# Transposes of x, dispatch and combine weights moved from TensorE to VectorE blocks and DMAs inside SBUF, in a kernel of attention and a soft mixture of experts

## The chip, the cores and the metric

The kernel runs on one core of one Trainium2 chip. The time is that of one execution on the device, in microseconds (us). All data are float32. A core has five engines that matter here: TensorE (PE, matrix products and transposes, results to PSUM), VectorE (DVE), ScalarE (ACT), GpSimd (POOL, hardly used) and SyncE (SP), whose queue starts all DMAs of this kernel.

## The reference

Attention without a softmax over 8 batches, and then a soft mixture of experts over all 19,968 tokens at once:

```python
scores = z @ z.transpose(0, 2, 1) / S              # B=8, S=2496, z has 64 columns
x = u * (np.maximum(scores, 0) ** 2 @ v)           # [8, 2496, 256] -> [19968, 256]
logits = x @ phi                                   # 32 slots: 8 experts of 4
d = softmax of logits over the tokens (axis 0)     # dispatch
slot_input = d.T @ x                               # [32, 256]
slot_out[e] = np.maximum(slot_input[e] @ w1[e], 0) @ w2[e]   # 256 -> 1024 -> 256
c = softmax of logits over the slots (axis 1)      # combine
out = c @ slot_out                                 # [19968, 256]
```

## The kernel before

**Attention loop.** The loop at L556 runs over 8 batches, 5 chunks of queries (four of 512 tokens and one of 448; the last batch starts with the 448 and ends with two of 256), and 5 steps of four key tiles (128 keys each). A step has two half-steps. `between(s)` (L560) opens a half-step: it takes one item from the list `work` (from the third half-step of a chunk on), then calls `pair` (L466), which issues the loads that are due and the scores of one pair of key tiles. `attend` (L215) follows with 24 matmuls into `acc` (22 and 20 in the last step, whose last key tile is half full).

**Scores and splits.** `scores` (L177) makes 6 matmuls into two PSUM tiles `sc` (a pool of two), since products of float32 are put together from high and low parts. ACT takes a relu of each into a tile `r` (a pool of four) and squares it there; DVE copies `r` rounded to `ph`, and subtracts: `pl` = `r` - `ph`. The tiles `ph` and `pl` (pools of ten) are what `acc` consumes. After the first 14, scores run three half-steps ahead of the `acc` matmuls that use them. The raw z and v of the next batch are loaded in the third to fifth chunk of a batch, and split into high and low parts by ACT and DVE a little later, in the lists `behind` (after the splits of a half-step) that `scores` runs.

**Groups.** When a chunk ends, `finish_chunk` (L263) multiplies `acc` by u into `xg` (x, features by tokens). At every 1024 tokens it adds a group, the generator `groups(q)` (L296), to `work`: 19 groups in the loop. A group makes the logits `lg` on PE, adds the slot sums of the group before (`late`), makes `L` (logits) and `E` (their exponentials, for dispatch) by DVE and ACT, turns x in 32 PE transposes of 64x64 (`turn_x`, L281, two items, copied to `xt` by ACT) and then L and E in 8 transposes (`le`). From `le` DVE and ACT make the combine weights `cw`; `slot_sums` (L381) multiplies the turned E by `xt`. Each group's slot sums are made with the logits of the next one; the last group of the loop (q = 18) makes its own.

**Order.** PE, ACT and DVE run in the order in which the program is written: their instructions go through `InOrder` (L42), so that each of them shows L50 as its line. SP's DMAs are called directly on `nc.sync`, and a scheduler places them.

**End.** In the last three half-steps `between_last` (L523) turns `cw` of 24 blocks (`cT`, L414 and L516) and the first part of the last 512 tokens' x. Behind the loop come the last 512 tokens, 15 transposes of the other `cw` blocks between them as fillers, the expert layers (`layer1`, `layer2`), and `tokens` (L818), which makes the output and sends it by DMA.

Of the kernel before, what the change touches and what calls it, by code (L numbers as in the profile page):

```python
# [53 lines left out]
def attn_soft_moe_kernel(ctx, tc, uT, v, zz, phi, ww, outT):  # L54
    nc = tc.nc

    pe, act, dve = (InOrder(tc, x) for x in (nc.tensor, nc.scalar, nc.vector))
# [17 lines left out]
    def load_z(b, j):  # L75
        if b == 0:
            raw = cw[:, 19 + 4 * j : 23 + 4 * j].rearrange("p g n -> p (g n)")
        else:
            raw = raws.tile([P, 512], F32, tag="raw", name=f"zr_{b}_{j}", bufs=NRAW)
        nc.sync.dma_start(raw, zz[b, :, j * 512 : (j + 1) * 512])  # L80
        zraw[b, j] = raw

        def split():
            t = zt[b, j] = blk.tile([P, 2, 512], F32R, tag="blk", name=f"z_{b}_{j}")
            for h in (1, 0):
                rows = HALF[h]
                act.copy(t[rows, h], raw[rows])
                dve.tensor_sub(t[rows, 1 - h], raw[rows], f32(t[rows, h]))

        return split  # L90

    def load_v(b, i):
        raw = raws.tile([P, 2, D], F32, tag="raw", name=f"vr_{b}_{i}", bufs=NRAW)
        nc.sync.dma_start(raw, v[b, :, 2 * i : 2 * i + 2, :])
# [27 lines left out]

    xt = xpool.tile([P, 2, 4, D], F32, name="xt")
# [3 lines left out]
    def constants():  # L127
# [13 lines left out]
        nc.sync.dma_start(phi_sb, phi.rearrange("(c p) s -> p c s", p=P))  # L141
# [35 lines left out]
    def scores(b, ch, p, w):  # L177
# [85 lines left out]
    def finish_chunk(b, ch, acc):  # L263
# [3 lines left out]
        while s < n:  # L267
# [13 lines left out]
    def turn_x(ps, x, j, ts):  # L281

        for t in ts:
            for c in range(2):
                for h, rows in enumerate(HALF):
                    pe.transpose(
                        ps[:, h, t * P + c * 64 : t * P + (c + 1) * 64],
                        x[rows, c, (4 * j + t) * P : (4 * j + t + 1) * P], ident[rows, rows],
                    )
        t = slice(ts[0], ts[-1] + 1)  # L290
        act.copy(
            xt[:, j, t].rearrange("p t (h k) -> p h t k", h=2),
            ps.rearrange("p h (t k) -> p h t k", k=P)[:, :, t],
        )

    def groups(q):  # L296
# [38 lines left out]
        yield  # L335
        if q == NQG - 2:

            yield

        for j in range(2):  # L340
            ps = ms_ps.tile([P, 2, 512], F32, tag="ms", name=f"tr_{q}_{j}")
            turn_x(ps, x, j, range(4))
            yield

        ps = ms_ps.tile([P, 2, 512], F32, tag="ms", name=f"le_{q}")
        for k, m_ in enumerate((L, E)):
            for j in range(2):
                for h, rows in enumerate(HALF):
                    o = (2 * k + j) * 64
                    pe.transpose(  # L350
                        ps[:, h, o : o + 64], m_[rows, j * P : (j + 1) * P], ident[rows, rows]
                    )
        le = wk.tile([P, 2, 2, P], F32, tag="le", name=f"le_{q}")
        lx, px = le.rearrange("p k j (h b) -> p h (k j) b", h=2), ps.rearrange("p h (k b) -> p h k b", b=64)
        act.copy(lx, px[:, :, 0:4])
        rm = wk.tile([P, 2, 8], F32, tag="rm", name=f"rm_{q}")
        lt = le[:, 0].rearrange("p j (t s) -> p (j t) s", s=NS)
        cg = cw[:, 2 * q : 2 * q + 2]
        cs = cg.rearrange("p j (t s) -> p (j t) s", s=NS)
# [4 lines left out]
        def combine():  # L364
            dve.tensor_reduce(rm[:, 0], lt, axis=AX.X, op=ALU.max)
            dve.tensor_sub(cs, lt, spread(0))
            middle.append(combine_exp)

        def combine_exp():
            act.activation(cg, cg, AF.Exp)  # L370
            begin.append(combine_sum)

        def combine_sum():
            dve.tensor_reduce(rm[:, 1], cs, axis=AX.X, op=ALU.add)
            dve.tensor_scalar_add(rm[:, 1], rm[:, 1], 1e-9)
            dve.reciprocal(rm[:, 1], rm[:, 1])
            dve.tensor_mul(cs, cs, spread(1))

        begin.append(combine)

        def slot_sums(ps):  # L381
            for j in range(2):
                for t in range(4):
                    e = le[:, 1, j, t * NS : (t + 1) * NS]
                    for h, rows in enumerate(HALF):
                        pe.matmul(
                            ps[t * NS : (t + 1) * NS, h, 0:D], e[rows], xt[rows, j, t],
# [18 lines left out]


        if q < NQG - 2:
            late.append(slot_sums)
            return  # L410
        yield
        slot_sums(ms_ps.tile([P, 2, 512], F32, tag="ms", name=f"sl_{q}"))

    def turn(k, ps):  # L414

        for i in range(min(8, NG - 8 * k)):
            for h, rows in enumerate(HALF):
                pe.transpose(ps[h][:, i * 64 : (i + 1) * 64], cw[rows, 8 * k + i], ident[rows, rows])
# [3 lines left out]
    def halves(t, g=8):  # L422
        return t[:, :g].rearrange("p g (h n) -> p h g n", h=2)

    def split_hi(k, px):
        n = min(8, NG - 8 * k)
        hi = blk.tile([P, 8, P], F32R, tag="blk", name=f"ch_{k}")
        act.copy(hi[:, :n], px[:, :n])
        parts[k] = hi, px

    def split_lo(k):
        n = min(8, NG - 8 * k)
        hi, px = parts[k]
        lo = blk.tile([P, 8, P], F32R, tag="blk", name=f"cl_{k}")
        dve.tensor_sub(lo[:, :n], px[:, :n], f32(hi[:, :n]))
        parts[k] = hi, lo


    def load_w(pool, tag):
        i = len(w_raw)  # L440
        if i < NW:
            t = pool.tile([P, 2, 512], F32, tag=tag, name=f"w_{i}")
            nc.sync.dma_start(t, ww[i].rearrange("p (k n) -> p k n", k=2))
# [5 lines left out]
    def load_u(b, ch):  # L449
# [3 lines left out]
        nc.sync.dma_start(  # L453
# [62 lines left out]
    def turn_out(k, ps):  # L516

        turn(k, ps)
        c8 = cw[:, 8 * k : 8 * k + 8]
        for h, copy in enumerate((act.copy, dve.tensor_copy)):  # L520
            copy(halves(c8)[:, h], ps[h].rearrange("p (g n) -> p g n", g=8))

    def between_last(k):  # L523
# [3 lines left out]
        if k:  # L527
            turn_x(xps[0], xg_[NQG - 1], 0, range(k - 1, k))
        if k == 1:
            ps = acc_ps.tile([P, 2, QC], F32, tag="acc", name="cT_1")  # L530
            turn_out(1, [ps[:, h] for h in range(2)])
        else:
            turn_out(k, [sc_ps.tile([P, QC], F32, tag="sc", name=f"cT_{k}_{h}") for h in range(2)])
# [65 lines left out]
    L = wk.tile([P, 2 * P], F32, tag="L", name="L_last", bufs=1)[:, 0:P]  # L599
    E = wk.tile([P, 2 * P], F32, tag="E", name="E_last", bufs=1)[:, 0:P]  # L600
    nc.gpsimd.memset(tiny[:, 0:512], 0.0)
# [7 lines left out]

    turned = [acc_ps.tile([P, 2, QC], F32, tag="acc", name="cT_3")]  # L610
    fills = iter(range(14))

    def turn_c8(i):
        pe.transpose(
            turned[i // 8][:, i // 4 % 2, i % 4 * P : (i % 4 + 1) * P], cw[:, 24 + i], ident
        )

    def fill(n):
        for i in [next(fills) for _ in range(n)]:
            turn_c8(i)  # L620
# [5 lines left out]
    def turn_c(c):  # L626

        for t in range(2):
            pe.transpose(xq[:, c, t * P : (t + 1) * P], x[:, c, (2 + t) * P : (3 + t) * P], ident)

    def copy_c(c):
        act.copy(
            xt[:, 0, 2:4].rearrange("p t (h c q) -> p t h c q", h=2, c=2)[:, :, :, c],
            xq[:, c, 0 : 2 * P].rearrange("p (t h q) -> p t h q", t=2, h=2),
        )
# [11 lines left out]
    turn_c(0)  # L647
    turn_c(1)
# [3 lines left out]
    act.activation(E, lg[:, 0:P], AF.Exp, bias=mneg[:, 0:1])  # L652
    copy_c(0)
    copy_c(1)
    dve.tensor_copy(L, lg[:, 0:P])
# [5 lines left out]
    fill(2)  # L661
    ps = acc_ps.tile([P, 2, QC], F32, tag="acc", name="et_last")
    turned.append(ms_ps.tile([P, 2, 512], F32, tag="ms", name="cT_4"))
    pe.transpose(ps[:, 0, 0:P], E, ident)
    act.copy(ET, ps[:, 0, 0:P])

    act.activation(fac, mneg, AF.Exp, scale=-1.0, bias=mtop)
    fill(3)
    lT = pm[:, P : 2 * P].rearrange("p (t s) -> p t s", s=NS)
    pe.transpose(pm[:, P : 2 * P], L, ident)  # L670
    fill(3)
    for t in range(4):
        pe.matmul(
            ps[t * NS : (t + 1) * NS, 1, 0:D], ET[:, t * NS : (t + 1) * NS], xt[:, 0, t],
            start=True, stop=True,
        )
    act.copy(snew[:, 0:D], ps[:, 1, 0:D])
    dve.tensor_reduce(snew[:, D : D + 1], E, axis=AX.X, op=ALU.add)
    dve.tensor_mul(
        fsel, ssel.unsqueeze(1).to_broadcast([P, 2, NS]), fac.unsqueeze(2).to_broadcast([P, 2, NS])  # L680
    )


    sums = [lg[:, 2 * P : 2 * P + NS], ps[:, 0, 2 * P : 2 * P + NS]]
# [8 lines left out]
    fill(2)  # L693

    cg = cw[:, NG - 1]
    cs = cg.rearrange("p (t s) -> p t s", s=NS)
# [4 lines left out]
    dve.tensor_reduce(rm[:, 0], lT, axis=AX.X, op=ALU.max)  # L701
    dve.tensor_sub(cs, lT, spread(0))
    slots(snew, 0)
    for c in range(2):
        dve.tensor_copy(
            sT[:, c, :, 0:SE], sums[c].rearrange("p (e s) -> p e s", s=SE)
        )
    act.activation(cg, cg, AF.Exp)


    tot = pm[:, 2 * P : 2 * P + NS]
# [6 lines left out]
    dve.tensor_reduce(rm[:, 1], cs, axis=AX.X, op=ALU.add)  # L718
    dve.tensor_scalar_add(rm[:, 1], rm[:, 1], 1e-9)
    dve.reciprocal(rm[:, 1], rm[:, 1])  # L720
    dve.tensor_mul(cs, cs, spread(1))
# [44 lines left out]
    whole = [cw[:, 8 * k : 8 * k + 8] for k in range(3)]  # L766
    whole += [t.rearrange("p h (g n) -> p (h g) n", n=P) for t in turned]
    hs = {}
    split_hi(3, whole[3])
    for i, k in enumerate((0, 1, 2, None)):  # L770
# [129 lines left out]
```

## Time and profile before

| | |
|---|---|
| median of 3 runs | 1495.19 us (1494.81 to 1495.38) |
| profiled execution | 1497.05 us |
| its span in the trace | 1495.1 us |
| end of the last `acc` matmul of the loop | 1418.6 us into the span |
| mean granted TensorE clock | 0.986 |

The page's slices show where the stages lie. Each digit is the busy share of one fortieth of the span (37.4 us) in tenths, and PEclk is the granted TensorE clock in tenths:

```profile
PE   9999999999999999999999999999999999999985
DVE  6878776887678777787778787687767787676754
ACT  7777766867567766777667766686767777665653
PEclk9999999999999999999999999999999999999995
DMA  4112201121001110121101120011101131000589
```

The loop fills 38 of the 40 slices. The last one and a half are the tail, in which the DMAs of the output are busiest. In the list of waits a row names who waits, for whom, the total in us, how often, and the longest; in a timeline a row has the start, the length, the engine, the line, the operation with output and inputs, and in brackets the idle time ahead of it with what ended it. A group's row has the total busy time and the mean in ns behind the first bar, and the idle time of the engine just ahead of it behind the second.

### The profile page before, as it was taken

To read this page: it belongs to the slowest core of one execution; us is meant where nothing else is said; L and a number is where in the kernel's file an instruction comes from. 1 tells how busy PE (TensorE), PEld (TensorE's weight loads), DVE (VectorE), ACT (ScalarE), POOL (GpSimd) and SP (SyncE) were. 2 spreads that over 40 slices of the span, in tenths; PEclk is the share of its full clock that TensorE was granted. 3 is DMA by queue.
4 is the path that set the end of the run, shared out by engine and by line. 5 is a ranking of instruction groups with operands and counts; after the bars stand their busy time and mean duration, and the time that the engine had idled before them with its cause. 6 is when DMAs were issued, how large, how long until landed. Compare 5 with 4: busy or idle time off the path is not lost.

```text
span 1495.1 us, 36884 instructions
## 1 busy us (share of the span) xinstructions
PE 1468.8 (98%) x14763; PEld 1247.3 (83%) x14763; DVE 1108.0 (74%) x2194; ACT 1025.1 (69%) x1982; POOL 3.7 (0%) x22
## 2 busy tenths in 40 slices
PE   9999999999999999999999999999999999999985
PEld 7888888889888888889988888888988889988952
DVE  6878776887678777787778787687767787676754
ACT  7777766867567766777667766686767777665653
POOL 0000000000000000000000000000000000000000
PEclk9999999999999999999999999999999999999995
DMA  4112201121001110121101120011101131000589
GB/s 133 31 30 58 55 24 29 30 64 57 16 23 51 50 42 15 30 55 51 30 16 43 52 70 16 15 51 49 51 16 30 51 112 56 16 16 23 191 317 388
DMA packets 36651, 91.53 MB, mean 61 GB/s; under 512 B 3712, under 2 KB 6272, under 8 KB 34432
## 3 DMA queue, kind: packets, MB, share of 16 engines
q1 hardware_dynamic: 36480, 89.18, 18.9%
q8 instruction: 116, 1.90, 0.6%
q14 instruction: 55, 0.45, 0.1%
HBM read 68.71 MB, written 20.45 MB: 60 GB/s over the span
## 4 chain that ended last, share of the span: by engine, by line
PE 97%; DMA 1%; ACT 1%; DVE 0%; issue 0%; SPq 0%; ACTq 0%; DVEq 0%
PE acc L50 71%; PE sc L50 19%; PE lg L50 2%; PE tr L50 1%; PE pf L50 1%; DMA outT<-ot 1%; PE po L50 1%; ACT ot L50 1%; PE h L50 0%; DMA vr<-in_v 0%; PE le L50 0%; PE cT L50 0%; DVE ot L50 0%; PE idle L50 0%; PE hT L50 0%
## 5 line engine op out<-in xcount | busy, mean ns | idle before, releaser
L50 PE MATMUL acc<-ph,v 64*128 64x512 f32 (+2 forms) x6396 | 1012.9, 381 | 0.4 <-issue 0.4
L50 PEld LDWEIGHTS acc<-ph,v 64*128 64x128 f32 x6396 | 653.2, 184 | 91.3 <-issue 0.8
L50 ACT ACTIVATE r<-sc 128x512 f32<-128x512 f32 (+2 forms) x820 | 429.1, 575 | 357.7 <-PE sc L50 351.7
L50 PE MATMUL acc<-pl,v 64*128 64x512 f32 (+2 forms) x3198 | 669.2, 380 | 0.0
L50 DVE TENSOR_TENSOR pl<-r,ph 128x512 fp32r<-128x512 f32 (+5 forms) x820 | 546.4, 666 | 68.3 <-PE acc L50 0.9
L50 DVE CAST ph<-r 128x512 fp32r<-128x512 f32 (+2 forms) x820 | 335.6, 409 | 249.5 <-ACT r L50 247.6
L50 ACT ACTIVATE r<-r 128x512 f32<-128x512 f32 (+2 forms) x820 | 454.9, 610 | 0.0
L50 PEld LDWEIGHTS acc<-pl,v 64*128 64x128 f32 x3198 | 347.2, 184 | 46.1
L50 PE MATMUL sc<-z,z 64*128 64x512 f32 (+2 forms) x1920 | 277.0, 384 | 0.2 <-ACT r L50 0.2
L50 PEld LDWEIGHTS sc<-z,z 64*128 64x128 f32 x1920 | 186.9, 185 | 32.5 <-issue 6.6
L50 PE MATMUL sc<-z 64*128 64x512 f32 (+2 forms) x480 | 69.9, 386 | 0.0
L50 DVE TENSOR_TENSOR v<-vr,v 128x512 fp32r<-128x512 f32 x80 | 54.9, 686 | 5.6 <-ACT v L50 5.2
L50 ACT COPY xt<-tr 128x1024 f32<-128x1024 f32 x38 | 38.6, 1016 | 27.2 <-PE tr L50 27.1
L50 PEld LDWEIGHTS sc<-z 64*128 64x128 f32 x480 | 47.0, 185 | 7.0 <-issue 1.6
L50 ACT CAST v<-vr 128x512 fp32r<-128x512 f32 x80 | 49.4, 617 | 3.7 <-DMA vr<-in_v 3.7
L50 DVE TENSOR_TENSOR xg<-acc,ut 128x1024 f32<-128x1024 f32 (+7 forms) x57 | 48.8, 880 | 1.2 <-PE acc L50 1.2
L50 DVE TENSOR_TENSOR z<-zr,z 64x512 fp32r<-64x512 f32 x70 | 48.0, 686 | 2.0
L50 ACT CAST z<-zr 64x512 fp32r<-64x512 f32 x70 | 43.4, 620 | 1.7
L50 DVE COPY ot<-pf 128x1024 f32<-128x1024 f32 (+2 forms) x22 | 24.3, 1104 | 23.1 <-PE pf L50 21.4
L50 ACT COPY ot<-pf 128x1024 f32<-128x1024 f32 (+2 forms) x22 | 20.1, 915 | 27.3 <-PE pf L50 22.4
L50 PE MATMUL pf<-ch,soh 32*128 32x512 f32 (+2 forms) x88 | 23.1, 570 | 12.4 <-ACT ot L50 12.4
L50 PEld LDWEIGHTS pf<-ch,soh 32*128 32x128 f32 x88 | 10.2, 244 | 23.1 <-ACT ot L50 22.1
(129 smaller groups left out, 449.1 us busy)
## 6 DMA issues: line engine op xcount, KB each, us to landing
vr<-in_v SPq DMA_DIRECT2D x80, 256.0 KB, 2.7
w<-in_w SPq DMA_DIRECT2D x32, 512.0 KB, 6.4
outT<-ot SPq DMA_DIRECT2D x16, 1024.0 KB, 7.0
ut<-in_uT SPq DMA_DIRECT2D x31, 512.0 KB, 3.7
zr<-in_zz SPq DMA_DIRECT2D x35, 256.0 KB, 2.7
ut<-in_uT SPq DMA_DIRECT2D x8, 448.0 KB, 3.5
outT<-ot SPq DMA_DIRECT2D x4, 512.0 KB, 4.5
outT<-ot SPq DMA_DIRECT2D x2, 768.0 KB, 7.2
```

Source lines behind the costliest of these rows:

```text
L50: return lambda *a, **k: self.tc.keep_in_program_order(f(*a, **k))
```

## The change

PE makes none of the loop's transposes any more, nor those of `cw`. DVE's transpose turns each 32x32 block of a tile in its place within a row of blocks, and 16 small DMAs (`shift`) then carry the blocks from one quarter of the partitions to another. This is done to E (tile `e1`, shifted to `es`) and to each half of x (tile `y`, a single buffer that both halves use in turn, shifted to `xt`). The logits are turned by DVE alone into `lt`; the combine softmax is made there in another order of tokens, and a second DVE transpose puts the result back into `cw`, in the layout that the end needs, so `turn`, `turn_out` and `turn_c8` go. A group now takes 8 items of `work` in place of 7 (14 for q = 18). The tiles `e1`, `es`, `lt` and `y` are new, and the pool of `r` has three buffers in place of four. SP's DMAs go through `InOrder` too, so they are issued in program order. Rows of w1 are permuted on the host to fit the new order of features.

```diff
-    pe, act, dve = (InOrder(tc, x) for x in (nc.tensor, nc.scalar, nc.vector))
+    pe, act, dve, sp = (InOrder(tc, x) for x in (nc.tensor, nc.scalar, nc.vector, nc.sync))
...
-            r = wa.tile([P, QC], F32, tag="r", name=f"r_{t0}_{k0 + h}", bufs=4)
+            r = wa.tile([P, QC], F32, tag="r", name=f"r_{t0}_{k0 + h}", bufs=3)
...
-                work.extend([lambda it=it: next(it, None)] * 7)
+                work.extend([lambda it=it: next(it, None)] * (14 if q == NQG - 2 else 8))
...
+    def shift(dst, src, n):
+        for a in range(4):
+            for b in range(4):
+                sp.dma_start(
+                    dst[32 * b : 32 * b + 32, a * n : (a + 1) * n],
+                    src[32 * a : 32 * a + 32, b * n : (b + 1) * n],
+                )
...
-        for j in range(2):
-            ps = ms_ps.tile([P, 2, 512], F32, tag="ms", name=f"tr_{q}_{j}")
-            turn_x(ps, x, j, range(4))
-            yield
-        ps = ms_ps.tile([P, 2, 512], F32, tag="ms", name=f"le_{q}")
...
-                    pe.transpose(
-                        ps[:, h, o : o + 64], m_[rows, j * P : (j + 1) * P], ident[rows, rows]
-                    )
...
+        e1 = wk.tile([P, 2 * P], F32, tag="e1", name=f"e1_{q}", bufs=1)
+        es = wk.tile([P, 2 * P], F32, tag="es", name=f"es_{q}", bufs=1)
+        def turn_e():
+            dve.transpose(
+                e1.rearrange("p (b j s) -> p j b s", b=4, j=2), E.rearrange("p (j b k) -> p j b k", j=2, b=4)
+            )
+            shift(es, e1, 64)
+        behind.append(turn_e)
         yield
...
+        def turn_block(y, j, c):
+            dve.transpose(
+                y.rearrange("p (b t c f) -> p c t b f", b=4, t=4, c=2)[:, c],
+                x[:, c, 512 * j : 512 * (j + 1)].rearrange("p (t b k) -> p t b k", t=4, b=4),
+            )
+            if c:
+                shift(xt[:, j].rearrange("p t d -> p (t d)"), y, D)
...
         def combine():
-            dve.tensor_reduce(rm[:, 0], lt, axis=AX.X, op=ALU.max)
-            dve.tensor_sub(cs, lt, spread(0))
-            middle.append(combine_exp)
+            dve.transpose(lt, L)
+            dve.tensor_reduce(rm[:, 0], l8, axis=AX.X, op=ALU.max)
+            dve.tensor_sub(l8, l8, spread(0))
...
+        def combine_turn():
+            dve.transpose(cw[:, 2 * q : 2 * q + 2].rearrange("p j n -> p (j n)"), lt)
...
+                            es[rows, o : o + NS],
+                            xt[rows, j].rearrange("p g (t n) -> p t g n", t=4)[:, t],
...
+        for j in range(2):
+            y = wk.tile([P, 2 * QC], F32, tag="y", name=f"y_{q}_{j}", bufs=1)
+            for c in range(2):
+                behind.append(lambda: turn_block(y, j, c))
+                if j:
+                    middle.append(combine_exp) if c == 0 and not short else None
+                yield
+            if j == 0:
+                if not short:
+                    behind.append(combine)
+                yield
+        if not short:
+            behind.append(combine_sum)
+            behind.append(combine_turn)
             late.append(slot_sums)
             return
...
-            turn_out(k, [sc_ps.tile([P, QC], F32, tag="sc", name=f"cT_{k}_{h}") for h in range(2)])
+            turn_x(xps[0], xg_[NQG - 1], k - 1)
+            copy_x(act.copy, xps[0], k - 1)
...
+    def fill(n, ps=ep_):
+        for _ in range(n):
+            pe.transpose(ps[:, 1, 0:P], ident, ident)
...
+    dve.transpose(cw[:, NG - 1], lt)
...
-    w1 = inputs["moe_w1"].reshape(2, 4, 2, 2, 64, 2, 512).transpose(0, 5, 3, 1, 2, 4, 6)
+    w1 = inputs["moe_w1"].reshape(2, 4, 2, 2, 2, 32, 2, 512).transpose(0, 6, 3, 1, 4, 2, 5, 7)
```

Three places of the order, all in the chunk that works off the first group. On PE before, the transposes of x stand between two half-steps (`acc` matmuls of key tile 7, then `tr`, then the scores of tiles 14 and 15):

```order
L50 MATMUL acc_1190<-pl_7_1213,v_3_272 128x512 x2
L50 MATMUL tr_0_1415<-ident,xg_691 128x64 x16
L50 MATMUL sc_14_1433<-z_2_568,z_3_665 128x512
L50 MATMUL sc_15_1434<-z_2_568,z_3_665 128x512
...
L50 MATMUL acc_1190<-ph_8_1255,v_4_321 128x512 x4
```

On PE now the same place has nothing between them:

```order
L50 MATMUL acc_1190<-pl_7_1213,v_3_272 128x512 x2
L50 MATMUL sc_14_1437<-z_2_568,z_3_665 128x512
L50 MATMUL sc_15_1438<-z_2_568,z_3_665 128x512
...
L50 MATMUL acc_1190<-ph_8_1255,v_4_321 128x512 x4
```

The row of 16 transposes is gone. On DVE now, from half-step 5 (key tiles 16 and 17) to half-step 7 (key tiles 0 and 1 of the next chunk), `y_0` and `y_1` being the two halves of the group's x in the same buffer:

```order
L50 STREAM_TRANSPOSE y_0_1436<-xg_691 128x4x4x32
L50 TENSOR_TENSOR z_1_1460<-zr_1_1240,z_1_1460 64x512 x2
L50 CAST ph_16_1505<-r_16_1500 128x512
...
L50 STREAM_TRANSPOSE y_0_1436<-xg_691 128x4x4x32
L50 CAST ph_18_1569<-r_18_1564 128x512
...
L50 STREAM_TRANSPOSE lt_1434<-L_1306 128x256
...
L50 TENSOR_TENSOR pl_1_1635<-r_1_1624,ph_1_1633 128x512
L50 STREAM_TRANSPOSE y_1_1611<-xg_691 128x4x4x32
L50 CAST ph_2_1676<-r_2_1671 128x512
```

The transposes stand behind the splits of one half-step and ahead of the first cast of the next, where before there were only splits, sums and subtractions; the first `y_1` row writes the buffer that the DMAs of `y_0` read. On SP now, from the last load ahead of the group to the first load behind it (`zr` and `vr` are z and v of the next batch, `ut` is u):

```order
L50 DMA zr_2_1368<-in_zz 128x512
L50 DMA es_1367<-e_0_1366 32x64 x16
L50 DMA zr_3_1490<-in_zz 128x512
L50 DMA xt<-y_0_1436 32x256 x16
L50 DMA zr_4_1612<-in_zz 128x512
L50 DMA xt<-y_1_1611 32x256 x16
L50 DMA vr_0_1730<-in_v 128x512
L50 DMA ut_1783<-in_uT 128x2x512
```

Three shifts of 16 DMAs have come between the loads, which stood directly behind each other there before; loads behind a shift in this queue are issued after it.

More of the change, by code (lines that the diff above doesn't have):

```diff
@@ L140, in constants @@
                 )
-        nc.sync.dma_start(phi_sb, phi.rearrange("(c p) s -> p c s", p=P))
+        sp.dma_start(phi_sb, phi.rearrange("(c p) s -> p c s", p=P))
         nc.gpsimd.memset(one, 1.0)
@@ L514, in attn_soft_moe_kernel @@
     xps = []
[L516 to L521, printed above, removed]
     def between_last(k):
@@ L607, in attn_soft_moe_kernel @@
     dve.tensor_scalar_mul(mneg[:, 1:2], mold, -1.0)
[L610 to L620, printed above, removed]
     lg = sc_ps.tile([P, QC], F32, tag="sc", name="lg_last")
@@ L624, in attn_soft_moe_kernel @@
     xq = ms_ps.tile([P, 2, 512], F32, tag="ms", name="tr_last_1")
[L626 to L635, printed above, removed]
+    ep_, tp = (acc_ps.tile([P, 2, QC], F32, tag="acc", name=n) for n in ("et_sums", "et_last"))
+    def fill(n, ps=ep_):
+        for _ in range(n):
+            pe.transpose(ps[:, 1, 0:P], ident, ident)
     def logits(c):
@@ L660, in attn_soft_moe_kernel @@
     )
[L661 to L665, printed above, removed]
+    pe.transpose(tp[:, 0, 0:P], E, ident)
+    act.copy(ET, tp[:, 0, 0:P])
     act.activation(fac, mneg, AF.Exp, scale=-1.0, bias=mtop)
-    fill(3)
-    lT = pm[:, P : 2 * P].rearrange("p (t s) -> p t s", s=NS)
-    pe.transpose(pm[:, P : 2 * P], L, ident)
+    dve.transpose(lt, lg[:, 0:P])
+    dve.tensor_mul(
+        fsel, ssel.unsqueeze(1).to_broadcast([P, 2, NS]), fac.unsqueeze(2).to_broadcast([P, 2, NS])
+    )
     fill(3)
@@ L692, in attn_soft_moe_kernel @@
     slots(sold, 1)
[L693 to L696 removed]
+    fill(2, tp)
+    l4 = lt.rearrange("p (b s) -> p b s", s=NS)
     def spread(i):
         return rm[:, i].unsqueeze(2).to_broadcast([P, 4, NS])
[L701 to L702 removed]
+    dve.tensor_reduce(rm[:, 0], l4, axis=AX.X, op=ALU.max)
+    dve.tensor_sub(l4, l4, spread(0))
     slots(snew, 0)
[L704 to L711, printed above, removed]
+    for c, copy in enumerate((dve.tensor_copy, act.copy)):
+        copy(sT[:, c, :, 0:SE], sums[c].rearrange("p (e s) -> p e s", s=SE))
+    act.activation(lt, lt, AF.Exp)
+    tot = tp[:, 0, 2 * P : 2 * P + NS]
     for z, k in (sold, 1), (snew, 0):
@@ L763, in layer2 @@
                 )
-    whole = [cw[:, 8 * k : 8 * k + 8] for k in range(3)]
-    whole += [t.rearrange("p h (g n) -> p (h g) n", n=P) for t in turned]
     hs = {}
-    split_hi(3, whole[3])
-    for i, k in enumerate((0, 1, 2, None)):
-        if k is not None:
-            split_hi(k, whole[k])
-        split_lo((3, 0, 1, 2)[i])
+    split_hi(0)
+    for i in range(4):
+        if i < 3:
+            split_hi(i + 1)
+        split_lo(i)
         hs[divmod(i, 2)] = layer1(*divmod(i, 2))
```

118 lines of the change are left out of this document (46 added, 72 removed).

## The prediction

> **What bounds the kernel now.** I read the page's engine line first, then the busy time by stage, then the chain that ended last.
>
> ```profile
> PE 1468.8 (98%) x14763; PEld 1247.3 (83%) x14763; DVE 1108.0 (74%) x2194; ACT 1025.1 (69%) x1982; POOL 3.7 (0%) x22
> 200.00:600.00 400.00, 400.00 (x3882) 339.10 (x3880) 298.69 (x589) 277.46 (x532) 0.00 (x0) 1.00 0.13 35
> PE 97%; DMA 1%; ACT 1%; DVE 0%; issue 0%; SPq 0%; ACTq 0%; DVEq 0%
> ```
>
> TensorE (PE) is busy 400.00 of 400.00 us at a granted clock of 1.00, and holds 97% of the chain. A TensorE instruction that goes is a saving, as long as the engines that feed it stay ahead. How far ahead they are decides this case, so the next rows are one beat of the loop: PE from the chain, then ScalarE (ACT), then VectorE (DVE).
>
> ```profile
> 382.06 0.69 PE sc L50 x6
> 382.76 2.79 PE acc L50 x24
> 385.55 0.69 PE sc L50 x6
> 382.57 1.09 ACT L50 ACTIVATE r<-sc 128x512 f32<-128x512 f32 x2 [1.35 <-PE sc L50]
> 383.54 1.15 ACT L50 ACTIVATE r<-r 128x512 f32<-128x512 f32 x2
> 384.21 0.43 DVE L50 CAST ph<-r 128x512 fp32r<-128x512 f32 x1 [1.12 <-ACT r L50]
> 384.74 0.69 DVE L50 TENSOR_TENSOR pl<-r,ph 128x512 fp32r<-128x512 f32 x1
> 385.35 0.42 DVE L50 CAST ph<-r 128x512 fp32r<-128x512 f32 x1
> 385.87 0.69 DVE L50 TENSOR_TENSOR pl<-r,ph 64x512 fp32r<-64x512 f32 x1
> ```
>
> A half-step (hs) is 3.49 us (382.06 to 385.55). DVE starts it 2.15 us in, and its two pairs take 2 x 1.14 = 2.27, so 1.2 us of each half-step are free. How late may DVE run? A relu takes a buffer r that an earlier subtraction frees. The second relu normally starts 1.0 us into its half-step, takes 0.6, and must end before the next scores, 3.49 in, since those reuse its PSUM bank: it may start 2.8 in. With three buffers (after) it waits for the first subtraction of the half-step before, which ends 3.37 after that one's start, 0.1 before this one begins. **DVE may be 2.9 us late with three buffers.** With four (before) it waits for the second subtraction of two half-steps before, which ended 2.4 us before this half-step begins (385.87 + 0.69 is 4.5 after its own start, and two half-steps are 7.0): 5.3 us. This run used more than 2.9:
>
> ```profile
> ACT r L50 <- DVE pl L50: 2.4, 5, 1.1
> 360.93 0.18 PE sc L50
> 358.96 0.41 DVE L50 TENSOR_REDUCE rm<-cw 128x8 f32<-128x256 f32 x1
> 360.20 0.42 DVE L50 CAST ph<-r 128x512 fp32r<-128x512 f32 x1
> 365.34 1.08 DVE L50 TENSOR_TENSOR xg<-acc,ut 128x896 f32<-128x896 f32 x1
> 366.34 0.42 DVE L50 CAST ph<-r 128x512 fp32r<-128x512 f32 x1
> ```
>
> The first row (the waits: total, count, longest) says that relus waited for a subtraction 2.4 us in the whole run. The casts for the scores of 360.93 were due at 363.1 and began at 366.34, 3.2 us late, without a gap on PE. (358.96 to 360.20 are the sums of a group's combine weights, 1.24 us.) With three buffers that alone would hold PE up.
>
> **What goes.** The transposes of the loop, and those of the last three half-steps:
>
> ```profile
> L50 PE MATMUL tr<-ident,xg 64*128 64x64 f32 x608 | 25.4, 222 | 0.0
> L50 PE MATMUL le<-ident,E 64*128 64x64 f32 x76 | 5.8, 223 | 0.0
> L50 PE MATMUL le<-ident,L 64*128 64x64 f32 x76 | 5.7, 218 | 0.0
> L50 PE MATMUL cT<-ident,cw 64*128 64x64 f32 x48 | 2.0, 223 | 0.0
> L50 ACT COPY xt<-tr 128x1024 f32<-128x1024 f32 x38 | 38.6, 1016 | 27.2 <-PE tr L50 27.1
> ```
>
> 25.4 + 5.8 + 5.7 = 36.9 us of PE, 1.94 for each of 19 groups, all on the path; cT adds 1.5 (its rows overlap neighbours). **38.4 us go.** The copies leave ACT, which waits 1.35 us a half-step anyway: nothing. The 15 large transposes after the loop give way to as many filling ones: nothing.
>
> **What comes.** Per group, on DVE: four transposes of 128x512 and three of 128x256. No row shows one. The nearest are a cast (0.42 us) below and two passes of a subtraction (1.2) above. I take one subtraction, 0.61 to the next start, 0.35 for the small ones, because both read one element after another and write one.
>
> ```profile
> L50 DVE TENSOR_TENSOR v<-vr,v 128x512 fp32r<-128x512 f32 x80 | 54.9, 686 | 5.6 <-ACT v L50 5.2
> L50 DVE TENSOR_TENSOR cw<-le,rm 128x256 f32<-128x256 f32 x19 | 8.1, 425 | 0.6
> L50 DVE TENSOR_REDUCE rm<-le 128x8 f32<-128x256 f32 x19 | 7.9, 414 | 0.2
> L50 DVE TENSOR_TENSOR slot_acc<-slot_acc,lg 128x256 f32<-128x256 f32 x18 | 7.5, 415 | 0.0
> L50 DVE SCALAR_TENSOR_TENSOR slot_acc<-slot_acc,m,lg 128x256 f32<-128x256 f32 x17 | 8.1, 474 | 0.0
> L50 DVE TENSOR_TENSOR xg<-acc,ut 128x1024 f32<-128x1024 f32 x19 | 23.1, 1218 | 0.0
> ```
>
> On SP: three shifts of 16 small DMAs, 912 in all. SP's queue is in program order, and the second `y` block (hs 7, VectorE) cannot be written until the first one's sixteen DMAs (issued after hs 5) have landed. Behind that instruction stand DVE's casts, and behind those ACT's relus and PE's scores. What an issue and a landing cost:
>
> ```profile
> 2.58 0.91 SPq L94 DMA_DIRECT2D vr<-in_v  x2
> 3.53 0.91 SPq L80 DMA_DIRECT2D cw<-in_zz  x2
> 343.63 0.33 SPq L94 DMA_DIRECT2D vr<-in_v  x1
> vr<-in_v SPq DMA_DIRECT2D x80, 256.0 KB, 2.7
> ut<-in_uT SPq DMA_DIRECT2D x31, 512.0 KB, 3.7
> phi_sb<-in_phi SPq DMA_DIRECT2D x1, 32.0 KB, 3.2
> ```
>
> Back to back an issue takes 0.475 us (2.58 to 3.53, two); alone 0.33 and a gap of 0.045. The ends are 0.375 and 0.475; sixteen in a row are nearest to the second, a little less for a quarter of the partitions: 0.45. Landing: 3.7 against 2.7 is 1 us for 256 KB, so 16 or 32 KB land in 1.8; phi, behind others, took 3.2. I take 2.1. **A shift then holds SP 7.2 us and lands 15 x 0.45 + 2.1 = 8.85 after its first issue.**
>
> The row says that 16 or 32 KB cost SP what 256 KB cost. The Trainium skill, "DMA: Bandwidth & Descriptors", section "Rules for kernel authors", would coalesce many small transfers into one, those under 64 KB being mostly overhead; it speaks against this change, and the trace's equal issue times agree.
>
> The groups run on hs 2 to 9 of a chunk. Lags at the first cast, carried on as lag + work - length (hs 8 and 9 have 22 and 20 matmuls: 3.25 and 3.02 us):
>
> *No splits beside it* (chunks of 512, seven groups). The E transpose ends 4.8 into hs 3, so SP is taken until 5.0 into hs 5; the first block's second half ends 5.0 into hs 5, so it lands 6.9 into hs 7. DVE comes there at 2.15 + 2.27 = 4.4 and **waits 2.5**. Lag 1.9 at hs 8; + 2.27 + 0.61 - 3.25 = 1.5 at hs 9; + 2.27 + 1.24 (the sums) + 0.35 - 3.02 + 1.15 (xg) = 3.5 at the next chunk's first cast. That is 0.6 over 2.9.
>
> *Beside z splits* (1.2 us in every second hs; four groups). Lag 1.0 at hs 3 with add_up (1.0), so E ends at 5.75, SP is free 6.4 into hs 5 with a load between, landing 8.3 into hs 7; DVE is there at 5.7, waits 2.6. Lags 3.3, then 4.1, then 6.1: 3.2 over.
>
> *Beside v splits in a 448-wide chunk* (four groups).
>
> ```profile
> 164.53 0.60 PE sc L50 x6
> 165.13 2.47 PE acc L50 x24
> ```
>
> Half-steps of 3.07, DVE's pairs 2.06. The shifts do not shrink: landing 8.7 into hs 7, DVE there at 5.2, wait 3.5. Lags 4.6, 5.1, 7.3: 4.4 over. The three groups beside v splits in 512-wide chunks, and the one in batch 7's 448-wide chunk, come between: 2.5.
>
> While ACT waits for r, two squares stand between it and DVE's next cast, 0.15 us a half-step for about four: 0.6 more, half of it in the lightest groups. Stalls: 6 x 0.9 + 4 x 3.8 + 4 x 3.1 + 4 x 5.0 = 53.
>
> *The last group* runs in 256-wide half-steps:
>
> ```profile
> 1403.25 1.40 PE acc L50 x24
> 1404.64 0.53 PE sc L50 x6
> ```
>
> Here 16 issues last four half-steps of 1.9. From the E transpose in hs 4 the first x shift lands 12.2 into hs 8, where DVE stands 3.0 in: it waits 9, of which PE has 1.0 to spare. The second shift then ends 2.4 after PE wants its sums: 10.5 together.
>
> Sum: 53 + 10.5 - 38.4 = +25. The profiled execution took 1497.05 us (span 1495.1 and 2.0 around it), 1.9 above the median; against the median the forecast is **1495.2 + 25 = 1520 us**. Time behind the loop stays: the output transfers end it as now.
>
> **Rivals.** *Cheap issues.* With 0.375 and 1.8, shifts land 1.4 us earlier and SP is free 1.2 earlier. The waits become 1.1, 0.5 and 0.95; the stalls 0, 1.5 and 2.4, 1 between, 8 at the end: 27.6 - 38.4 = -11, **1484**. For it: a quarter of the partitions. Against: 32 KB of phi kept SP as long as its neighbours.
>
> *Hidden altogether* (the other side): if an issue costs so little that SP never holds a shift up, no wait is left; only the extra work with three buffers stalls, 4 x 1.2 + 4 x 0.85 + about 4: -26, **1469**. It decides from an issue of about 0.3 us down, below every row. A sentence of the Trainium skill, same page, section "Issuing engines are not separate DMA queues", holds the sequencer's time for starting a DMA "usually small relative to the DMA itself"; by it this rival would win, and 0.33 us against a landing of 2.7 bears it out only for single large loads.
>
> *Dearer.* Transposes at 1.2 us add about 2.5 a group, **1567**; landings of 3.2 with issues of 0.475 add 1.9, **1554**. The program has the transposes on DVE and none of the loop's on PE, so that the change does nothing of the sort is out.
>
> **How the numbers follow.** Forecast 0.56 (1503 to 1545), dearer 0.18, cheap issues 0.18, hidden 0.08. Slower by over 0.2% (3 us, about what a measurement of this kernel can tell) is 0.56 + 0.18 + a little of the cheap case: 0.75. Within: 0.05. Faster: 0.20. The range of 8 in 10 reaches into the cheap and the dear case: 1482 to 1562.
>
> **What would show it.** SP's shifts of sixteen at 0.4 to 0.5 us an issue; a wait of DVE for DMA at y, some 2 to 4 us, 19 times; ACT's relus waiting for pl (now 2.4 us in all) by tens of us; PE's scores waiting for r; a last chunk some 10 us longer. A PE that stays at 400 of 400 would prove the forecast wrong, as would transposes near 0.42 with landings under 1.8.

## The result, and the profile after

The changed kernel takes **1685.43 us** (median of 5 runs, 1683.54 to 1686.82) beside 1494.81 us for the kernel before: a ratio of 1.1279, with a 95% interval of 1.1266 to 1.1292. It is 190.6 us slower. The forecast was 1520 us, with a range from 1482 to 1562: the sign was right, the size was not near.

The page of the changed kernel: the engines' busy time, the clock by slices, the chain that ended last, two groups, and two kinds of DMA with their median time from issue to landing.

```profile
span 1681.6 us, 36566 instructions
PE 1501.9 (89%) x13945; PEld 1268.3 (75%) x13945; DVE 1176.3 (70%) x2324; ACT 985.7 (59%) x1923; POOL 3.8 (0%) x22
PEclk9999899898989999989999999989999999999795
PE 71%; SPq 12%; DVE 6%; DMA 4%; issue 3%; ACT 3%; DVEq 0%; ACTq 0%; POOLq 0%
L50 DVE STREAM_TRANSPOSE y<-xg 128x512 f32<-128x512 f32 x76 | 53.7, 707 | 173.2 <-DMA xt<-y 173.2
L50 ACT CAST v<-vr 128x512 fp32r<-128x512 f32 x80 | 49.3, 616 | 58.9 <-DMA vr<-in_v 58.9
xt<-y SPq DMA_DIRECT2D x608, 32.0 KB, 1.9
es<-e SPq DMA_DIRECT2D x304, 8.0 KB, 1.8
```

PE's share of the chain fell from 97% to 71%, and SP's queue, which held nothing, now holds 12%. No engine became busy: DVE went from 1108.0 to 1176.3 us, and is at 70% of the longer span. What came is waiting. Behind the second bar of the transposes' row stands the idle time just ahead of them, 173.2 us, all of it for the DMAs that read `y`. ACT's casts of v wait 58.9 us for loads, where the same row of before had 3.7:

```profile
L50 ACT CAST v<-vr 128x512 fp32r<-128x512 f32 x80 | 49.4, 617 | 3.7 <-DMA vr<-in_v 3.7
```

The list of waits has the same in another form (total, times, longest):

```profile
ACT r L50 <- DVE pl L50: 178.4, 79, 16.6
DVE y L50 <- DMA xt<-y: 173.2, 19, 15.8
PE sc L50 <- ACT r L50: 152.4, 31, 15.9
ACT v L50 <- DMA vr<-in_v: 58.9, 17, 9.2
```

The 19 waits at `y` are one for each group, 9.1 us each. Relus wait for subtractions (178.4 us, 2.4 before), and scores for relus: the path that the prediction named, `y` to casts to relus to scores, with waits three times as long.

One group in a chunk without loads shows where they come from. First SP's queue (start, length, and how many DMAs stand in one row), then DVE, then PE:

```profile
611.07 10.93 SPq L50 DMA_DIRECT2D es<-e  x16
622.11 17.97 SPq L50 DMA_DIRECT2D xt<-y  x20
633.81 0.71 DVE L50 STREAM_TRANSPOSE y<-xg 128x512 f32<-128x512 f32 x1 [7.90 <-DMA xt<-y]
634.45 0.39 DVE L50 CAST ph<-r 128x512 fp32r<-128x512 f32 x1
636.39 1.22 PE L50 MATMUL sc<-z 64*128 64x512 f32 x4 [6.47 <-ACT r L50]
```

The sixteen DMAs of E hold SP from 611.07 to 622.00, 0.68 us each in the mean, and the sixteen of x's first half follow at once (the row of twenty takes in the first four of the second half, issued from 637.41 on). The last one of the first half goes out some ten microseconds after 622.11 and lands about 1.9 later; at 633.81 DVE may write `y`. It had nothing else to do for 7.90 us, because the casts for PE stand behind that transpose. PE stood for 6.47.

### The profile page after: what moved, and what is told of

Its sections match the earlier page's. It is cut to its first block, busy times and chain, and to the rows that moved or that the text cites. A ratio compares the mean times of both kernels' runs of the same rounds, so it can differ in the third digit from the quotient of the medians.

```text
span 1681.6 us, 36566 instructions
## 1 busy us (share of the span) xinstructions
PE 1501.9 (89%) x13945; PEld 1268.3 (75%) x13945; DVE 1176.3 (70%) x2324; ACT 985.7 (59%) x1923; POOL 3.8 (0%) x22
## 4 chain that ended last, share of the span: by engine, by line
PE 71%; SPq 12%; DVE 6%; DMA 4%; issue 3%; ACT 3%; DVEq 0%; ACTq 0%; POOLq 0%
PE acc L50 52%; PE sc L50 15%; SPq L50 12%; PE lg L50 2%; DMA xt<-y 2%; DVE pl L50 2%; ACT r L50 2%; DVE ph L50 2%; DMA vr<-in_v 1%; PE pf L50 1%; DMA outT<-ot 1%; DVE lt L50 1%; PE po L50 1%; ACT ot L50 1%; DVE rm L50 1%
## 5 line engine op out<-in xcount | busy, mean ns | idle before, releaser
L50 PE MATMUL acc<-ph,v 64*128 64x512 f32 (+2 forms) x6396 | 1109.8, 389 | 0.1
L50 PEld LDWEIGHTS acc<-ph,v 64*128 64x128 f32 x6396 | 810.0, 190 | 87.3 <-POOLq L251 0.5
L50 PE MATMUL acc<-pl,v 64*128 64x512 f32 (+2 forms) x3198 | 840.3, 387 | 0.0
L50 ACT ACTIVATE r<-sc 128x512 f32<-128x512 f32 (+2 forms) x820 | 439.2, 574 | 555.7 <-PE sc L50 366.4
L50 PEld LDWEIGHTS acc<-pl,v 64*128 64x128 f32 x3198 | 493.9, 189 | 44.6
L50 PE MATMUL sc<-z,z 64*128 64x512 f32 (+2 forms) x1920 | 329.9, 398 | 139.3 <-ACT r L50 138.8
L50 PEld LDWEIGHTS sc<-z,z 64*128 64x128 f32 x1920 | 224.7, 191 | 189.2 <-ACT r L50 154.8
L50 DVE STREAM_TRANSPOSE y<-xg 128x512 f32<-128x512 f32 x76 | 53.7, 707 | 173.2 <-DMA xt<-y 173.2
L50 PE MATMUL sc<-z 64*128 64x512 f32 (+2 forms) x480 | 79.7, 391 | 13.5 <-ACT r L50 13.4
L50 ACT CAST v<-vr 128x512 fp32r<-128x512 f32 x80 | 49.3, 616 | 58.9 <-DMA vr<-in_v 58.9
L50 PEld LDWEIGHTS sc<-z 64*128 64x128 f32 x480 | 53.8, 187 | 25.5 <-ACT r L50 18.3
L50 DVE TENSOR_TENSOR v<-vr,v 128x512 fp32r<-128x512 f32 x80 | 54.1, 677 | 10.7 <-ACT v L50 10.3
```

The source lines that it names most:

```text
L50: return lambda *a, **k: self.tc.keep_in_program_order(f(*a, **k))
```

## The experiments

Three statements were to be told apart: that SP's issues cost so much that the queue is the limit (the theory); that DVE's new work and the third `r` buffer cost most by themselves; and that the number or the traffic of small DMAs costs wherever they stand. The medians, and their ratios to runs of the kernel before taken beside them (1493.6 to 1494.7 us), were:

| run | us | ratio, 95% interval |
|---|---|---|
| e1, no shifts | 1490.79 | 0.9978 (0.9969 to 0.9988) |
| e2, second half of x three half-steps later | 1565.04 | 1.0493 (1.0462 to 1.0524) |
| e3, 12 DMAs a shift | 1576.71 | 1.0549 (1.0533 to 1.0565) |
| e4, before with 3 `r` buffers and SP in order | 1503.94 | 1.0065 (1.0050 to 1.0080) |
| e6, no shifts, 4 `r` buffers | 1468.65 | 0.9834 (0.9819 to 0.9848) |
| e7, spread shifts, last group on PE | 1476.44 | 0.9886 (0.9869 to 0.9902) |
| e8, the same with 4 `r` buffers | 1470.62 | 0.9851 (0.9835 to 0.9868) |
| e9, 44 fills on PE | 1684.86 | 1.1276 (1.1259 to 1.1293) |
| e10, the change with 4 `r` buffers | 1678.96 | 1.1241 (1.1223 to 1.1260) |
| e11, 66 fills on PE | 1683.06 | 1.1267 (1.1245 to 1.1288) |

For several of them the traces are read by chunk: the time from the first `acc` matmul of a chunk to that of the next, and for the last chunk to the end of its `acc` matmuls, in us. Worked out from the traces' PE rows:

| chunk (counted from 0) | before | after | e1 | e6 | e2 | e8 |
|---|---|---|---|---|---|---|
| 15, a group, no loads | 37.67 | 43.67 | 36.45 | 36.29 | 36.55 | 36.38 |
| 16, the next | 34.19 | 36.18 | 34.19 | 34.19 | 34.19 | 34.19 |
| 17, a group beside loads of z | 37.70 | 45.19 | 36.52 | 36.29 | 36.51 | 36.31 |
| 18, the next | 33.83 | 36.10 | 35.90 | 33.83 | 38.05 | 33.83 |
| 19, a group beside v, 448 wide | 33.89 | 44.20 | 33.01 | 32.53 | 44.05 | 32.55 |
| 20, the next | 34.19 | 35.61 | 35.58 | 34.19 | 35.72 | 34.19 |
| 40, the last | 19.68 | 40.53 | 20.71 | 21.00 | 39.31 | 19.19 |

**e1, no shifts.**

```diff
-        for a in range(4):
+        for a in range(0):
```

> The changed kernel without its 912 shift DMAs: es and xt are set to zero once at the start and never written, so the slot sums of the loop are zero; the seven DVE transposes of a group, the three buffers of r and SP's program order stay. Theory (SP: an issue of 0.63 us makes the second y block wait 9.1 us, and loads stand behind the shifts): without shifts no wait at y is left and PE runs at its own pace, 1495 less 38 of transposes plus about 12 for the late DVE, 1465 to 1480 us. Rival (the new DVE work and the third buffer cost most by themselves): above 1600.

Measured: 1490.79 us. With the shifts 194.6 us went. The rival, DVE's new work and the third buffer as the main cost, falls. But the time is 11 us above the upper end of what was expected: of the transposes' saving almost nothing is left. In the table a group's chunk is 0.9 to 1.2 shorter than before, and the next one up to 2.1 longer, so something takes the gain back without any DMA.

**e4, the frame.**

```diff
-            r = wa.tile([P, QC], F32, tag="r", name=f"r_{t0}_{k0 + h}", bufs=4)
+            r = wa.tile([P, QC], F32, tag="r", name=f"r_{t0}_{k0 + h}", bufs=3)
...
-        nc.sync.dma_start(
+        sp.dma_start(
```

> The kernel before with only two parts of the change: three buffers of r in place of four, and SP's DMAs in program order. Theory: DVE runs more than 2.9 us late in few places, so 1495 to 1503 us. Rival (the third buffer is what makes the changed kernel slow): above 1530.

Measured: 1503.94 us, 10.1 us slower, a little above the range. Three buffers (and SP's order) cost something even with DVE's old work.

**e6, no shifts and four buffers.** The edit of e1, and:

```diff
-            r = wa.tile([P, QC], F32, tag="r", name=f"r_{t0}_{k0 + h}", bufs=3)
+            r = wa.tile([P, QC], F32, tag="r", name=f"r_{t0}_{k0 + h}", bufs=4)
...
+        es = e1
```

> The kernel without shifts of before (the slot sums of the loop are made of the unshifted e1 and of zeros), with four buffers of r in place of three. Theory: without shifts the late DVE and the third buffer ate what the transposes gave, so with four buffers relus wait for a subtraction in all under 10 us in place of 68, and the time goes from 1490.8 to 1468 to 1479 us. Rival (DVE's extra work is late for the acc matmuls themselves, buffers or not): 1485 to 1491 us.

Measured: 1468.65 us. The fourth buffer is worth 22.1 us here. Relus wait for subtractions 20.6 us in all, more than expected, but PE no longer feels it: chunks 16, 18 and 20 take what they took before. So the full saving, DVE's new work paid for, is 1493.84 - 1468.65 = 25.2 us, and the third buffer gives back 22.1 of it where no shift is issued.

**e2, the second half of x later.**

```diff
+                for _ in range(0 if short else 3):
+                    yield
```

> The second half of x is turned three half-steps later (11 items of work a group in place of 8), all 912 shifts stay. Theory: the sixteen DMAs of the first half have landed by then, DVE's wait at y falls from 173 us to under 15; what is left is the loads of z and v behind the shifts on SP (ACT waited 68 us for them), partly hidden: 1500 to 1560 us. Rival (the traffic of the small DMAs, or their number on SP, binds the loop wherever they stand): the time stays above 1640.

Measured: 1565.04 us, 120.4 below the change, a little above the expected range. The waits of this run:

```profile
ACT v L50 <- DMA vr<-in_v: 67.5, 16, 9.0
DVE v L50 <- ACT v L50: 48.6, 16, 7.7
DVE y L50 <- DMA xt<-y: 14.8, 1, 14.8
```

Eighteen of the nineteen waits at `y` are gone with all 912 DMAs still there; so most of the cost is not their number or their traffic, but where they stand. Of the 75 us that the loop still takes longer than in e1, 61 stand in two places of the table: chunk 19 and its three like, where loads of v wait behind a shift (44.05 against 33.01 without shifts), and the last chunk (39.31), whose group was not moved. In the 448-wide chunks the change takes about as long as e2 (44.20 in chunk 19): there the wait at `y` and the wait for v run side by side, and taking away the first alone gained at most 0.4 us.

**e3, twelve DMAs a shift.**

```diff
-            for b in range(4):
+            for b in [b for b in range(4) if b != a]:
```

> The four DMAs of each shift that stay in their own quarter of the partitions are left out (36 instead of 48 a group; those parts of es and xt stay zero). Theory: the wait at y is made of issues of 0.633 us one behind the other; 4 fewer for E and 4 fewer for x bring it from 9.1 to about 9.1 - 8 x 0.633 = 4.0, so 19 x 5.1 = 97 us go, and some of the loads' wait: 1570 to 1595 us. Rival (DVE work and buffers): within 10 us of 1685. Rival (bytes and traffic): a quarter of the wait goes, 2.3 x 19 = 43, about 1640.

Measured: 1576.71 us. DVE's wait at `y` fell by 94 us, where eight issues of 0.633 for 19 groups are 96:

```profile
DVE y L50 <- DMA xt<-y: 79.0, 19, 10.1
ACT v L50 <- DMA vr<-in_v: 26.8, 7, 6.1
```

The wait goes with the number of issues ahead of it, E's included. A wait in proportion to bytes would have kept 130 us of it (three quarters of 173.2).

**e5, the price of an issue.** Extra DMAs in the frame kernel, in stretches where SP is idle, for example:

```diff
+        if (b, j) == (1, 1):
+            for r, g in cells:
+                sp.dma_start(bench[r, g], rs_[0:32])
+        if (b, j) == (2, 1):
+            for r, g in cells:
+                sp.dma_start(bench[r, g], v[0, 0:32, g])
```

> The frame kernel with DMAs added in stretches where SP is idle, to measure an issue by itself: 16 of 32x64 inside SBUF, 16 of 32x256 inside SBUF, 4 of 128x256 inside SBUF, 8 of 64x256 inside SBUF, 16 of 32x256 from DRAM, 4 of 128x256 from DRAM, 16 of 32x256 inside SBUF that keep their partitions; into a tile that nothing reads. Theory A (an issue inside SBUF costs 0.63 us, whatever its shape): the four kinds inside SBUF at 0.60 to 0.66 us from start to start, both kinds from DRAM at 0.45 to 0.50. Theory B (few partitions make it dear): everything of 32 partitions at 0.63, from DRAM too, and 128x256 inside SBUF at 0.45 to 0.50. Theory C (the other traffic of the changed kernel makes it dear): all at 0.45 to 0.50 here.

Measured, in SP's timeline (start, length of all, how many), in the order in which they run: 32x64, 32x256 and 128x256 inside SBUF, 32x256 and 128x256 from DRAM, 64x256 inside SBUF, and 32x256 inside SBUF on the same partitions.

```profile
192.52 11.17 SPq L50 DMA_DIRECT2D bench<-rsel  x16
225.44 10.02 SPq L50 DMA_DIRECT2D bench<-rsel  x16
368.14 3.44 SPq L50 DMA_DIRECT2D bench<-rsel  x4
401.12 8.83 SPq L50 DMA_DIRECT2D bench<-in_v  x16
541.07 1.88 SPq L50 DMA_DIRECT2D bench<-in_v  x4
578.91 4.96 SPq L50 DMA_DIRECT2D bench<-rsel  x8
721.03 10.04 SPq L50 DMA_DIRECT2D bench<-rsel  x16
```

From start to start the median inside SBUF is 0.633, 0.633, 0.645, 0.637 and 0.633 us, and from DRAM 0.463 and 0.475 (the rows at 192.52, 368.14 and 401.12 each hold one issue of 1.4 to 1.6). Theory A holds: the dear thing is neither the small piece nor the few partitions but that both ends lie in SBUF. 8 KB and 128 KB cost SP the same.

**e7 and e8, the queue packed anew.** The edit of e2, and: shifts put their DMAs into a list, from which each half-step issues four behind its loads; the last group of the loop (q = 18) is turned by PE as its half-steps are too short. e8 has four `r` buffers as well, with the turned logits in the memory of E.

```diff
+        drip(4)
...
-                sp.dma_start(
+                drips.append((
...
+        for j in range(2 if short else 0):
+            ps = ms_ps.tile([P, 2, 512], F32, tag="ms", name=f"tr_{q}_{j}")
...
-        lt = wk.tile([P, 2 * P], F32, tag="lt", name=f"lt_{q}", bufs=1)
+        lt = wk.tile([P, 2 * P], F32, tag="E", name=f"lt_{q}", bufs=1)
```

> The changed kernel with the second half of x turned three half-steps later, the shifts issued four DMAs to a half-step behind that half-step's loads, and the last group of the loop (q = 18) turned by PE; all is computed. Theory (only the packing of SP's queue was wrong): DVE's wait at y and ACT's wait for loads both under 10 us in all, the last chunks as without shifts, so about the time without shifts, 1484 to 1497 us. Rival (864 small DMAs cost by their number or traffic, wherever they stand): above 1520.

> The same with four buffers of r (the turned logits share E's memory). Theory: the late DVE no longer holds the relus up, so the transposes' saving of some 1.3 us a group shows: 1465 to 1482 us, faster than before and than the change. Rival (the buffers were not what held it): within 4 us of the run with three buffers.

Measured: 1476.44 and 1470.62 us. The waits of e8, in which 864 of the 912 DMAs are still issued:

```profile
DVE y L50 <- DMA xt<-y: 2.3, 2, 1.3
ACT v L50 <- DMA vr<-in_v: 3.0, 2, 2.1
```

e7 is faster than expected, and faster than e1, which has no shifts at all: relus wait for subtractions 30.5 us in all, where e1 had 67.8, and the chunks behind a group beside z are 1.8 to 2.0 us shorter. That turning the second half of x in the next chunk takes DVE's work off the crowded end of the group's own chunk fits this; no run has that move alone. e8 beats both kernels: 1.5% below before, and 2.0 us above e6. Once nobody waits for them, the small DMAs cost no more than that.

**e10, the change with four buffers.** The edits of e8 on `r` and `lt` alone.

> The changed kernel with four buffers of r in place of three (the turned logits share E's memory). Theory: a fourth buffer lets DVE be 2.4 us later in each group before PE stands, as without shifts, where it was worth 22 us; with 18 long waits up to 2.4 us each: 1640 to 1668 us. Rival (the waits of 9 us are so long that one buffer does not matter): 1680 to 1690 us.

Measured: 1678.96 us, 6.5 us less: outside both expected ranges. The rows show where the gain goes. First the gap of PE in chunk 7 of the change, then PE, ACT and PE again in this run:

```profile
319.78 1.64 PE L50 MATMUL sc<-z,z 64*128 64x512 f32 x5 [8.39 <-ACT r L50]
```

```profile
318.14 1.22 PE L50 MATMUL acc<-ph,v 64*128 64x512 f32 x4 [4.97 <-DVE ph L50]
334.32 0.62 ACT L50 CAST v<-vr 128x512 fp32r<-128x512 f32 x1 [3.31 <-DMA vr<-in_v]
335.49 1.44 PE L50 MATMUL sc<-z 64*128 64x512 f32 x6 [1.72 <-ACT r L50]
```

The relus may now run on, and PE stands some matmuls later and for less time, for `ph` itself: DVE's wait uses up the lead of the scores too. But then ACT waits for a load of v, issued at 331.33 right behind the second shift of x, and PE stands once more. Chunks 7 and 8 together take 81.3 us in place of 82.1. In the three groups in whose chunks no load waits (15, 25 and 37) the chunk and the next are 2.7 to 3.7 us shorter than in the change; elsewhere, but for chunk 35, little or nothing is gained, and ACT's waits for v come to 71.3 us in place of 58.9.

**e9 and e11, fills for the clock.** Behind each gap the granted clock is 0.50 for some microseconds, and PE's busy time is 1501.9 - 1450.4 = 51.5 us longer than in e1 for the same instructions. That looks like a cost of its own. Filling transposes of `ident`, whose result nobody uses, stand ahead of the scores that wait:

```diff
+            ps = ms_ps.tile([P, 2, 512], F32, tag="ms", name=f"fill_{q}")
+            for _ in range(44):
+                pe.transpose(ps[:, 0, 0:P], ident, ident)
```

> The changed kernel with 44 filling transposes of ident (about 5 us at full clock, 16 of them took 1.97 us behind the loop) on PE in each of 18 groups, just ahead of the scores that wait longest (gaps of 5.6 to 8.9 us); their results are not used. Theory (the half clock after each gap costs by itself: PE's busy time is 51 us longer than without shifts for the same instructions): with PE busy in the gap the clock stays up, and although work is added the time falls by 1 to 2 us a group, 1648 to 1672 us. Rival (the slow matmuls stand beside a DVE that is late anyway, so the clock costs nothing of its own): 1682 to 1700 us.

> As the run with 44 fills, with 66 (about 7.6 us): with 44 a gap of 2 to 5 us was left in each group and the clock behind it was 0.50 as before, so that run could not tell the theories apart. Theory (the half clock costs by itself): with gaps under about 2 us the clock behind them stays above 0.9 and the time falls by 1 to 2 us a group, 1648 to 1670 us. Rival (the clock costs nothing of its own, PE is paced by the late DVE behind the gap too): 1680 to 1700 us with the clock up.

Measured: 1684.86 and 1683.06 us, no change worth the name. With 44 a gap of over 1 us was left in fifteen of the eighteen groups, and the clock fell behind eleven, not behind all as the second expectation has it; with 66 hardly any is (0.6 us at 643.4 in the group shown, at most 3.5 elsewhere in the first eighteen groups). The same 12 us in windows (columns: length, then busy time and count of PE, PEld, DVE, ACT and POOL, then the clock, the share of the DMA engines and GB/s), for the change and for e11:

```profile
631.00:634.00 3.00, 0.00 (x0) 0.00 (x0) 0.19 (x1) 0.00 (x0) 0.00 (x0) 1.00 0.14 37
634.00:637.00 3.00, 0.61 (x4) 0.52 (x6) 2.79 (x6) 1.26 (x3) 0.00 (x0) 0.65 0.00 0
637.00:640.00 3.00, 3.00 (x18) 2.31 (x16) 2.76 (x7) 2.37 (x5) 0.00 (x0) 0.50 0.10 27
640.00:643.00 3.00, 3.00 (x22) 2.41 (x20) 2.86 (x7) 0.23 (x1) 0.00 (x0) 0.72 0.21 55
```

```profile
631.00:634.00 3.00, 3.00 (x27) 2.65 (x27) 0.46 (x1) 0.23 (x1) 0.00 (x0) 1.00 0.13 33
634.00:637.00 3.00, 3.00 (x27) 2.25 (x25) 2.79 (x6) 1.90 (x4) 0.00 (x0) 1.00 0.00 0
637.00:640.00 3.00, 3.00 (x30) 2.50 (x28) 2.72 (x8) 2.24 (x5) 0.00 (x0) 1.00 0.13 33
640.00:643.00 3.00, 3.00 (x29) 2.58 (x26) 2.90 (x6) 0.60 (x1) 0.00 (x0) 1.00 0.20 49
```

The clock stays at 1.00 (in the first eighteen groups of e11 it falls to 0.50 twice, for 3.4 us each), and from 634 us on DVE's busy times are the same to a tenth, 2.7 to 2.9 of 3 us in both: once it may go on it works almost without a pause, and PE follows it, at whatever clock. The theory of the clock as a cost falls; the low clock is a sign of the wait. The Trainium skill, "TensorE: Matmul & The Clock Gate", section "What's actually happening", has the clock at one half after an idle window of about 3.4 us and back at full after as long a busy one. The trace agrees with that much (0.50 from 637 to 640 us, behind a gap of 6.47 us; in the first eighteen groups each stretch at 0.50 lasts 3.4, 6.8 or 10.2 us), but here the time hangs on the engine that PE waits for.

## Why the prediction was wrong

**The step that failed** is the price of an issue: "The ends are 0.375 and 0.475; sixteen in a row are nearest to the second, a little less for a quarter of the partitions: 0.45". It is 0.633. Both ends came from loads out of DRAM, since the trace before has no DMA inside SBUF, and they were taken as bounds for another kind of DMA. e5 shows the kind alone to be the difference. So a shift holds SP 10.1 us and not 7.2, and the two shifts ahead of the second `y` block stand behind each other. The "dearer" rival went no further than 0.475, and so the range ended at 1562.

**What this does by the prediction's own steps.** With 0.633 and the landing measured at 1.9 (forecast 2.1), E's shift ends 2.9 us later, and x's last DMA lands 11.4 instead of 8.85 after its first issue: each wait grows by 5.45. The waits become 7.95, 8.05 and 9.0 us, and 14.5 for the last group. (Two slips of the prediction have no weight: E's DMAs carry 8 KB, not 16, and the groups without splits are six, as its sum has them, not seven.) Measured, by the brackets of DVE's timeline, are 7.0 to 7.9 in chunks without splits, 8.4 to 8.8 beside z, 9.7 to 10.7 beside v in 448-wide chunks, and 15.8 at the end. The mechanism, the queue and the place were right.

The stalls then are 53 + 18 x 5.45 = 151, and about 18 for the last group, whose second shift ends later as well; less 38.4 that is +131, some 1626 us. Of the other 59 us, the first two of these terms were measured:

- **The saving** was 38.4 and is 25.2 (e6). The step took the busy time of 1.94 us a group as path. The trace before had it otherwise, by the starts of the next rows:

```profile
341.25 0.69 PE L50 MATMUL tr<-ident,xg 64*128 64x64 f32 x16
341.71 0.89 PE L50 MATMUL sc<-z,z 64*128 64x448 f32 x6
344.86 0.67 PE L50 MATMUL tr<-ident,xg 64*128 64x64 f32 x16
345.32 0.88 PE L50 MATMUL sc<-z 64*128 64x448 f32 x6
348.48 0.30 PE L50 MATMUL le<-ident,L 64*128 64x64 f32 x4
348.59 0.31 PE L50 MATMUL le<-ident,E 64*128 64x64 f32 x4
348.69 0.67 PE L50 MATMUL sc<-z 64*128 64x448 f32 x4
```

  0.46 + 0.46 + 0.21 is 1.13 a group, 21.5 for 19: matmuls overlap, and a busy time holds the tail that the next one covers. The prediction saw this for `cT` alone. 13 us.

- **The third buffer** costs 22.1 us without shifts (e1 against e6); the rival "hidden altogether" had 4 x 1.2 + 4 x 0.85 + about 4 = 12 for the same. Beside z the chunk behind a group lost up to 2.1 us, not 1.2. 10 us.

- **The loads behind the shifts** were left out: the sum let them delay the shifts, not the shifts them. In the change ACT waits 58.9 us for v and 9.2 for z. In e2 these waits alone keep the four 448-wide chunks 10 to 11 us longer than without shifts. In the change they run beside DVE's wait there, and how much they add in all no run separates.

About 36 us are left for the loads and for what stays open. The loads can't be all of it: in the three groups in whose chunks no load waits (15, 25 and 37), the chunk and the next take 8.0 to 9.4 us more than in e6, where the prediction's steps with 0.633 give 0.9 + 5.45 = 6.4. Why these stalls are some 2 us longer is not shown.

**What was right:** the transposes' price (0.64 from 633.81 to 634.45, forecast 0.61), the landing, PE's stall by way of `r`, the worst place at the end of the loop, that SP's order and not the traffic decides, and that the change is slower. "Slower" had 0.75 of the chance.

Of the 190.6 us: -25.2 for the transposes gone from PE, +22.1 for the third buffer, +194.6 for the shifts (each a difference of two medians; the kernel before, measured beside each, agrees to within 1.0 us, which is why the three sum to 191.5). The shares hang on the order in which the parts are taken: with four buffers the shifts cost 1678.96 - 1468.65 = 210.3 us, and with the shifts the third buffer costs only 6.5.

## What to carry to other kernels

A bound read off one kind of DMA is no bound for another: where the trace has no row of the kind that a change adds, leave the upper end open, or measure that kind alone first, which took one run here. Before moving a pass off the busiest engine, write down whose queue it enters and who stands behind it there; here 48 issues of 0.63 us stood ahead of loads and of a buffer with one copy, and the cure was to issue four per half-step behind the loads, to use the buffer later, and to leave the last group of the loop to PE; the other 864 DMAs all stayed. Take what an instruction costs on a full engine from the start of the next one, not from its busy time.

## What the runs showed of the hardware that was not expected

An issue of a DMA with both ends in SBUF took SP 0.633 to 0.645 us from start to start, whether it moved 8 or 128 KB, over 32, 64 or 128 partitions; one from DRAM took 0.463 to 0.475 (e5). The Trainium skill, "DMA: Bandwidth & Descriptors", section "Issuing engines are not separate DMA queues", calls this time "usually small relative to the DMA itself"; for these it was a third of the 1.9 us to landing, and sixteen in a row took five times as long as one to land. A granted clock of 0.50 for several microseconds behind each gap, in 18 groups, cost nothing that could be measured here, where PE waited for DVE all the same: closing nearly all of the gaps with other work changed the time by 2.4 us of 1685.
